# The last 52 rows of two neighbouring Z blocks in one buffer, contracted two at a time

## The chip, the cores and the metric

The kernel runs on one core of one Trainium2 chip. The metric is the device time of one execution in microseconds (us), as the median of several. Runs of the kernel before gave 372.31 us (371.18 to 373.6, three runs). A difference of about 1% is what such a measurement tells from none.

The core has five engines that run their own instruction streams and wait for one another through semaphores. In the profile PE is the matrix engine (TensorE), PEld its weight loads, DVE the vector engine, ACT the scalar engine, POOL the GpSimd engine, and SP the engine that only issues DMAs here. Matrix products are written to PSUM, eight banks of 512 fp32 columns, and read from there by DVE and ACT.

## The reference

Eight batches of 5696 positions and 128 channels go through a long convolution, done with Fourier transforms, and then through a spectral mixing layer with 64 modes:

```python
Yf = rfft(x, n=2*S, axis=1) * rfft(h, n=2*S, axis=0)[None]
x  = irfft(Yf, n=2*S, axis=1)[:, :S, :]
X  = rfft(x, axis=1)
Yr = einsum(Xr, w_r) - einsum(Xi, w_i)          # the first 64 modes alone
Yi = einsum(Xr, w_i) + einsum(Xi, w_r)
y  = irfft(Y, n=S, axis=1)
u  = x + y
out = u + maximum(u @ w_ch, 0)
```

Inputs and output are fp32; the kernel works in fp16 with fp32 sums.

## The kernel before

The length 5696 is written as 89 x 64 (NQ x J). The transforms are matrix products with constant tables in two steps. The batches go in four groups of two (`g_`).

**First part, 0 to 249 us.** For each group, PE makes a first transform over the 89 (`a_tile`, buffers As), then in ticks of four frequencies a second one over the 64 (`second`: matmuls that contract 64 rows, the two batches on partitions 0-63 and 64-127 in turn, `As,M`; the filter's own are `Ah,M`). DVE multiplies by the filter (`products`, U), PE transforms back one step (`U,Wc`), ACT copies the result to Zs or Zt, and SP stores it to a scratch in HBM (`zscr`). Matmuls `G,Zs` take the 64 modes from the same data. `modes` and `second` follow one another in each tick.

**Second part, the output stage, 249 us to the end.** The scratch is read back in 16 Z blocks, four for each group. A block holds, for 16 of the 64 inner positions, all 2 x 90 = 180 rows of frequency (real and imaginary) of two batches: 128 rows of 8 KB go to a buffer ZTa (1024 KB), the 52 rows 128 to 179 to partitions 32 to 83 of a buffer ZTb (416 KB). Partitions 0 to 31 of ZTb are cleared by POOL (`clear_zt`), since those matmuls contract partitions 0 to 83 with the first 32 zero. There are five rooms of such pairs (`NC = 5`); block i + 5 is sent for (`load_zt`, on SP's queue) when the last tile of block i has been issued (b equal to 1).

A Z tile (`u_tile`, `u_z`) is half a block of one batch and fills two PSUM banks of 356 columns. For each bank PE runs one matmul of 356 columns (`u_c`: the mixing layer's share, `IBs,C`), and then four times one of 128 rows (`S4a,ZTa`) and one of 84 rows (`S4b,ZTb`), each 89 columns. ACT or DVE then copies both banks to UT. There are 64 such tiles. Between them stand the result tiles (`o_tile`): four matmuls of 256 columns with the channel weights (`WI,UT`), a ReLU on ACT (R), a sum on DVE (O), and, after every second one as a rule, a DMA of 512 KB to the output. O has seven rooms of 512 KB, used in turn, and four smaller ones. All loads of Z and all stores of results go through SP's one queue, in program order.

Which order the instructions have is written out by hand. During the last group's ticks a table `early` says at which tick a load is issued: tick 8 loads the table S4b, 10 block 0, 12 S4a, 14 the table IBs, 16 block 1, 19 block 3, 21 block 2; block 4 follows at the end. Only the first 33 of 64 columns' groups of S4a, S4b and IBs are loaded; the rest is made from them on the chip (`reflect`, lines 545 to 552: S4a and IBs on DVE, S4b on ACT). Three Z tiles (block 0) are run without their `IBs,C` matmuls ahead of time, between the matmuls of the mixing layer (`mix`).

All matmuls have line 323 in the profile (the helper `mm`), all DMAs line 320, ACT's copies line 311, DVE's line 315.

Of the kernel before, what the change touches and what calls it, by code (L numbers as in the profile page):

```python
# [4 lines left out]
P = 128  # L5
# [118 lines left out]
def bass_long_conv_fft__then__afno_spectral_mix_kernel(nc, x, h, moe_w_r, moe_w_i, moe_w_ch, out):  # L124
# [37 lines left out]
    s4t = np.zeros((P, 2 * SH))  # L162
    s4t[:, 0:SH] = rows[0:P, 0:SH]
    s4t[PB:PB + RB, SH:2 * SH] = rows[P:2 * NK, 0:SH]
    sg = np.ones((P, 3))
    sr = np.stack([(-1.0) ** kk, -(-1.0) ** kk], axis=1).reshape(2 * NK)
    sg[:, 0] = sr[0:P]
    sg[PB:PB + RB, 1] = sr[P:2 * NK]
    sg[M:P, 2] = -1.0
    tt = np.arange(S)  # L170
# [79 lines left out]
    wc_sb = at("Wc", 2 * P, F16, take(2 * P * 2))  # L250
    sg_sb = at("SG", 3, F32, take(12))
# [4 lines left out]
    ZB = 16  # L256
# [4 lines left out]
    zt_off = [(a_h, a_h2), (a_as1, a_as1 + 2 * ZP), (a_as1 + 4 * ZP, a_as1 + 6 * ZP), (a_h + 2 * ZP, a_h2 + 2 * ZP),  # L261
              (a_m2, a_g)]
    assert 2 * S + 8 * ZP <= AW * 2
    zt = [[at(f"ZT{i}{'ab'[p_]}", ZP, F16, zt_off[i][p_]) for p_ in range(2)] for i in range(NC)]
    ib_sb = at("IBs", S, F16, a_m)
    s4_sb = [at("S4a", S, F16, a_m + 2 * S), at("S4b", S, F16, a_as)]
    assert 4 * S + 2 * ZP + 4 * P + 2048 <= 2 * MW
# [31 lines left out]
    def bank(i):  # L299
        return ("bank", i)  # L300
# [226 lines left out]
    ZX = [("zs", i, b) for i in range(NZ, NZL) for b in range(2)]  # L527
    zt_old = [(H_ALL, H_ALL), (AST, AST), (AST, AST), (H_ALL, H_ALL), (M_ALL[3:6], G_ALL)]

    def load_zt(i):  # L530
        g_, c_ = divmod(i, J // ZB)
        for part, (p0, r0, n) in enumerate(((0, 0, P), (PB, P, RB))):
            old = list(once(("zt", i % NC, part), zt_old[i % NC][part]))
            dma("sync", bass.AP(zt[i % NC][part], p0 * ZP, [[ZP, n], [1, ZP]]),
                bass.AP(zs, (g_ * 2 * NK + r0) * J * 256 + c_ * ZB * 256, [[J * 256, n], [1, ZP]]),
                "t", [("zd", g_, s_) for s_ in range(NT)], [("zt", i % NC, part)], after=old)

    def clear_zt(i):
        z32 = zt[i][1][0:PB, :].bitcast(U32)
        R.add("gpsimd", lambda e: e.memset(z32, 0), (), [("zt0", i)], after=list(zt_old[i][1]) + pace)  # L540

    def load_ib():
# [11 lines left out]
    def load_s4(part):  # L554
        n = PB + RB if part else P
        dma("sync", s4_sb[part][0:n, 0:SH], bass.AP(c_s4, part * SH, [[2 * SH, n], [1, SH]]), "p", (),
            [("s4", part, 0)], after=AST if part else M_ALL[1:4])
# [13 lines left out]
    pace = []  # L571

# [176 lines left out]
    for g_ in range(NP):  # L749
        if g_ == NP - 1:  # L750
            load_w(0)
            load_w(1)
        for t in range(NT + LM):
            tick(g_, t)
            assert g_ + 1 < NP or not wp
            if g_ == NP - 1 and t in early:
                pace[:] = [("u", min(t, NT - 1) % NU)]
                early[t]()
        evac(bass.AP(xt, 2 * g_ + B, [[B * XTW, P], [B, 2], [3 * B, M], [1, 2]]), pv(MB, 0, [[M, 2], [1, M], [P, 2]]),
             [bank(MB)], [("xt", g_)], 1.0 / 64, eng="scalar", after=[("ag", k) for k in range(NS + 2 * XN, NK)])  # L760
        evac(bass.AP(xt, 2 * g_, [[B * XTW, P], [3 * B, M], [1, 2]]), pv(MB, M, [[1, M], [P, 2]]),
             [bank(MB)], [("xtn", g_)], -1.0 / 64, eng="vector" if g_ + 1 == NP else "scalar", after=[("ag", k) for k in range(NS + 2 * XN, NK)])
        if g_ + 1 < NP:
            for j in range(NB_, 32):
                a_tile(j, [(0, 4, 2, 6)[(j - 5) % 4]], "both" if j == 31 else (A, V)[(j - NB_) % 9 % 2])
                if j == 31:
                    second(g_ + 1, 0, 0, DA)
                if wp and j % 2 == 1:
                    dst, src_, ring, tok = wp.pop(0)
                    dma("gpsimd", dst, src_, ring, (), [tok], after=[("as", j)])  # L770


    pace[:] = []
    load_wi()
    for i in range(4, NC):
        load_zt(i)
        clear_zt(i)

# [4 lines left out]

    def u_z(i, b, half, alone=False, parts=(0, 1)):
        g_, c_ = divmod(i, NCH)
        t = ahead.get((i, b, half))
        if t is None:
            t = turns("l", LSLOT)
        z = zt[i % NC]
        for hb in parts:  # L790
            if not alone:
                u_c(i, b, half, t, hb, True)
            for pl in range(4):
                for ri in range(2):
                    pz = half * 8 + hb * 4 + pl
                    so = (c_ * ZB + pz) * NQ
                    n = (P, PB + RB)[ri]
                    mm(pv(t + hb, pl * NQ, [[1, NQ]]), z[ri][0:n, pz * 256 + b * P:pz * 256 + b * P + P], s4_sb[ri][0:n, so:so + NQ],
                       alone and pl == 0 and ri == 0, not alone and pl == 3 and ri == 1, [("zt", i % NC, ri), ("zt0", i % NC), ("s4", ri, 0)] + ([("s4", ri, 1)] if c_ >= NCH // 2 else []), [bank(t + hb)])
        if alone:  # L800
            ahead[(i, b, half)] = t
        return t

    def u_c(i, b, half, t, hb, first_):
        g_, c_ = divmod(i, NCH)
        pl0 = half * 8 + hb * 4
        mm(pv(t + hb, 0, [[1, 4 * NQ]]), c_sb[:, (2 * g_ + b) * P:(2 * g_ + b + 1) * P],
           ib_sb[:, (c_ * ZB + pl0) * NQ:(c_ * ZB + pl0 + 4) * NQ], first_, not first_,
           [("c", g_ // 2), ("ib", 0)] + ([("ib", 1)] if c_ >= NCH // 2 else []), [bank(t + hb)])

    def u_tile(i, b, half):
        g_, c_ = divmod(i, NCH)
        t = ahead.get((i, b, half))
        if t is None:
            t = u_z(i, b, half)
        else:
            for hb in range(2):
                u_c(i, b, half, t, hb, False)
# [39 lines left out]
    reflect("vector", ib_sb, P, 2, ("ib",), M_ALL[0:2])  # L858

# [52 lines left out]
    todo = []  # L912
    NB = NCH * NP
    NW4 = NW // 4
    for g_ in range(NP):
        last = g_ == NP - 1
        order = [(c_, b) for b in range(2) for c_ in range(NCH)] if last else [(c_, b) for c_ in range(NCH) for b in range(2)]
        for n, (c_, b) in enumerate(order):
            i = NCH * g_ + c_
            for half in range(2):  # L920
                u_tile(i, b, half)
                for _ in range((2, 2 + half)[n >= NCH] if last else 1 + half):
# [4 lines left out]
            if last and n == NCH - 1:  # L927
                todo += [(g_, 0, r4) for r4 in range(NW4)]
# [37 lines left out]
```

## Time and profile before

| | value |
|---|---|
| median of three runs | 372.31 us |
| span of the profiled execution (first to last instruction) | 370.1 us |
| PE busy | 354.7 us (96%) |
| ACT busy | 316.2 us (85%) |
| DVE busy | 291.8 us (79%) |
| DMA, mean over the span | 281 GB/s |
| granted TensorE clock | 0.999 |
| Z tile evacuations, ACT and DVE | 46 of 752 ns, 18 of 892 ns |
| result stores O, 512 KB | 39, median 10.5 us from issue to landing |

The page and the trace are of one execution; the page gives its span and no separate total. A row of a timeline is: start in us from the span's first instruction, duration in us, engine, line, operation, output and inputs, shape and count; in brackets the engine's idle time before it and what ended that. Matmuls are pipelined and their ends are modelled, so what one costs is read from start to start. A row of DMA issues gives the count, the size of one in KB (1024 bytes) and the median time from issue to landing.

### The profile page before, as it was taken

Reading aid. Unit: us, or ns where it says so; the run is one execution under the profiler, and the core shown is the slowest. Engines: PE = TensorE matmul, PEld = TensorE weight load, DVE = VectorE, ACT = ScalarE, POOL = GpSimd, SP = SyncE. Lnnn points to the kernel's source line nnn. Section 1 sums busy time; section 2 is a strip of 40 time slices with the busy share of each in tenths; the row PEclk is TensorE's granted clock in tenths of the full one; section 3 lists DMA queues with packets and bytes.
Section 4 is the critical chain, followed back from the end, with each engine's and each line's share of the span. In section 5 each row is a group of like instructions: output and inputs, shape, how many; then the busy total and the mean of one; then the engine's idle time right before and its main releaser. Section 6 shows DMA issues by size and latency. Waiting matters only on the chain.

```text
span 370.1 us, 12455 instructions
## 1 busy us (share of the span) xinstructions
PE 354.7 (96%) x5350; PEld 276.5 (75%) x5350; DVE 291.8 (79%) x332; ACT 316.2 (85%) x499; POOL 75.2 (20%) x117
## 2 busy tenths in 40 slices
PE   7999899999999999999999999999999999999994
PEld 7878766667866668866668766668899888888873
DVE  3549899988999999989999988775357777756666
ACT  8559999999999999999999999995467777688885
POOL 8804012100833311823213001151000000000000
PEclk9999999999999999999999999999999999999999
DMA  7999979969999996999996999999999999999878
GB/s 139 209 271 382 249 165 292 232 198 283 93 140 213 263 258 186 132 160 215 263 278 128 171 310 363 342 345 388 381 410 386 413 410 408 418 399 376 326 291 349
DMA packets 87048, 103.94 MB, mean 281 GB/s; under 512 B 22730, under 2 KB 72522, under 8 KB 83438
## 3 DMA queue, kind: packets, MB, share of 16 engines
q1 hardware_dynamic: 64610, 81.33, 62.5%
q0 software_dynamic: 22384, 21.83, 35.4%
q8 instruction: 42, 0.69, 0.7%
q14 instruction: 12, 0.10, 0.1%
HBM read 70.61 MB, written 51.12 MB: 329 GB/s over the span
## 4 chain that ended last, share of the span: by engine, by line
PE 78%; ACT 10%; DMA 7%; DVE 3%; issue 1%; POOL 1%; DVEq 0%; POOLq 0%
PE ps L323 78%; ACT As L313 6%; DMA out_dram<-O 5%; DMA Hin<-in_h_dram 2%; ACT R L898 1%; DVE As L317 1%; ACT Xs L311 1%; DVE U L623 1%; POOL Hin L320 1%; ACT UT L311 1%; DVE O L899 0%; ACT Zs L311 0%; DVE Hp L438 0%; ACT C L313 0%; DVE Hs L315 0%
## 5 line engine op out<-in xcount | busy, mean ns | idle before, releaser
L652 DVE TENSOR_TENSOR U<-Xs,Hs 128x2048 f16<-128x2048 f16 (+1 forms) x72 | 85.8, 1197 | 12.1 <-ACT Xs L311 11.5
L323 PE MATMUL ps<-U,Wc 128*128 128x512 f16 (+1 forms) x368 | 93.8, 376 | 1.4 <-DVE U L623 1.4
L311 ACT CAST Xs<-ps 128x1024 f16<-128x1024 f32 (+1 forms) x76 | 75.0, 995 | 5.8 <-PE ps L323 3.1
L311 ACT CAST Zs<-ps 128x512 f16<-128x512 f32 (+1 forms) x132 | 70.1, 605 | 0.7
L899 DVE TENSOR_TENSOR O<-ps,R 128x512 f32<-128x512 f32 x81 | 52.4, 684 | 21.6 <-ACT R L898 11.4
L898 ACT ACTIVATE R<-ps 128x512 f32<-128x512 f32 (+1 forms) x92 | 50.5, 592 | 8.5 <-PE ps L323 8.4
L317 DVE TENSOR_SCALAR As<-ps 128x720 f16<-128x720 f32 x64 | 53.1, 879 | 4.8 <-PE ps L323 3.3
L323 PE MATMUL ps<-As,M 64*128 64x128 f16 (+3 forms) x1504 | 52.5, 214 | 2.4 <-ACT As L313 1.2
L313 ACT ACTIVATE As<-ps 128x720 f16<-128x720 f32 (+1 forms) x68 | 48.2, 771 | 5.0 <-PE ps L323 4.8
L323 PE MATMUL ps<-F,Xin 128*128 128x180 f16 x512 | 52.1, 249 | 0.1
L323 PE MATMUL ps<-WI,UT 128*128 128x256 f16 x360 | 50.8, 278 | 0.5 <-ACT UT L311 0.4
L311 ACT CAST UT<-ps 128x712 f16<-128x712 f32 x46 | 34.5, 752 | 19.4 <-PE ps L323 18.4
L323 PEld LDWEIGHTS ps<-U,Wc 128*128 128x128 f16 x368 | 29.1, 97 | 28.2 <-DVE U L623 1.9
L323 PEld LDWEIGHTS ps<-F,Xin 128*128 128x128 f16 x512 | 45.2, 155 | 6.7 <-DVE Xin L365 0.9
L323 PEld LDWEIGHTS ps<-As,M 64*128 64x128 f16 x1504 | 42.2, 94 | 8.7 <-ACT Xs L311 1.9
L323 PEld LDWEIGHTS ps<-WI,UT 128*128 128x128 f16 x360 | 38.9, 152 | 3.2 <-issue 1.8
L323 PE MATMUL ps<-IBs,C 128*128 128x356 f16 x128 | 39.2, 314 | 0.8 <-DVE O L899 0.7
L320 POOL DMA_DIRECT2D Xt<-in_x_dram x40 | 21.4, 540 | 76.5 <-PE ps L323 76.0
L323 PEld LDWEIGHTS ps<-G,Zs 128*128 128x128 f16 x512 | 26.1, 96 | 14.1 <-ACT Zs L311 0.2
L652 DVE TENSOR_TENSOR U<-ps,Hs 128x2048 f16<-128x2048 f32 (+1 forms) x16 | 35.5, 2216 | 0.0
L323 PE MATMUL ps<-G,Zs 128*128 128x128 f16 (+2 forms) x512 | 31.9, 192 | 0.1
L311 ACT CAST Zt<-ps 128x512 f16<-128x512 f32 x52 | 29.1, 659 | 0.0
(76 smaller groups left out, 479.4 us busy)
## 6 DMA issues: line engine op xcount, KB each, us to landing
out_dram<-O SPq DMA_DIRECT2D x39, 512.0 KB, 10.5
zscr<-Zs SPq DMA_DIRECT2D x62, 256.0 KB, 6.7
zscr<-Zt SPq DMA_DIRECT2D x26, 256.0 KB, 6.6
Xt<-in_x_dram POOLq DMA_DIRECT2D x20, 320.0 KB, 6.9
W<-wscr SPq DMA_DIRECT2D x4, 1024.0 KB, 8.5
ZT0a<-zscr SPq DMA_DIRECT2D x4, 1024.0 KB, 11.0
M<-cM POOLq DMA_DIRECT2D x5, 720.0 KB, 17.6
ZT1a<-zscr SPq DMA_DIRECT2D x3, 1024.0 KB, 11.1
```

The source lines that it names most:

```text
L311: R.add(e, lambda h_: h_.copy(dst, src), reads, writes, after=after)
L313: R.add(e, lambda h_: h_.activation(dst, src, COPY, scale=scale), reads, writes, after=after)
L317: R.add(e, lambda h_: h_.tensor_scalar_mul(dst, src, scale), reads, writes, after=after)
L320: R.add(eng, lambda h_: h_.dma_start(dst, src), reads, writes, ring=ring, after=after)
L323: R.add("tensor", lambda h_: h_.matmul(o, l, r, start=st, stop=sp), reads, writes)
L623: R.add("vector", lambda e: e.tensor_tensor(bass.AP(u_s[0], b * 512 + d0, [[2048, P], [1024, 2], [D, n], [1, d1 - d0]]), bass.AP(s_[0], s_ ...
L652: R.add("vector", lambda e: e.tensor_tensor(uv, src, hv, MULT), bk + [("h", t, 0), ("h", t, 1, 0), ("h", t, 1, J)], [("u", i)])
L898: R.add("scalar", lambda e: e.activation(rv, src_r, RELU), bk, [("r", i % NR)], after=once(("r", i % NR), G_ALL + XTT + [("y", 0), ("y", 1 ...
L899: R.add("vector", lambda e: e.tensor_tensor(ov, src_u, rv, ADD), bk + [("r", i % NR)], [key + (h_,)], after=once(key, old))
```

## The change

Blocks are handled in neighbouring pairs (2k and 2k + 1), `k` counting pairs. The 128-row parts have seven rooms of their own (ZA), the 52-row parts three rooms (ZB), each of which holds the 52 rows of both blocks of a pair: the even block's on partitions 0 to 51, the odd block's on 64 to 115. The table S4b is laid out to match, with all its columns loaded (128 partitions of 2848 columns, in place of 84 of 2937), and it isn't reflected any more. Nothing has to be cleared.

A tile now takes four inner positions of each of the two blocks, in place of eight of one. Its order on PE is: both `IBs,C` matmuls, the four 128-row matmuls of the first bank, the four of the second, and then four times one 52-row matmul of the even block into the first bank and one of the odd block into the second. The loads at a pair's end are both parts of ZB for pair k + 3 and ZA for blocks 2k + 7 and 2k + 8. In the early table, tick 10 sends for ZA0 and ZB0, 16 for ZA1, 19 for ZA2 and ZB1, 21 for ZA3; at the end follow ZA4, ZB2, ZA5 and ZA6. Result tiles stand at the same places between the tiles.

```diff
-    RB, PB = 2 * NK - P, 32
+    RB, PB = 2 * NK - P, 64
+    s4b = np.zeros((P, S // 2))
+    for p0 in range(2):
+        s4b[p0 * PB:p0 * PB + RB] = rows[P:].reshape(RB, J // ZB // 2, 2, ZB * NQ)[:, :, p0].reshape(RB, S // 2)
...
-    NC = 5
+    NCA, NCB = 7, 3
...
+    za_off = [a_h, a_as1, a_h + 2 * ZP, a_as1 + 4 * ZP, a_as1 + 6 * ZP, a_m2, a_g]
+    zb_off = [a_h2, a_h2 + 2 * ZP, a_as1 + 2 * ZP]
...
+    def load_za(i):
+        g_, c_ = divmod(i, J // ZB)
+        r_ = i % NCA
+        dma("sync", za[r_][:, :], bass.AP(zs, g_ * 2 * NK * J * 256 + c_ * ZP, [[J * 256, P], [1, ZP]]),
+            "t", zdone(g_), [("za", r_)], after=once(("za", r_), za_old[r_]))
+
+    def load_zb(k):
+        r_ = k % NCB
+        for p0 in range(2):
+            g_, c_ = divmod(2 * k + p0, J // ZB)
+            n = RB - RS
+            dma("sync", bass.AP(zb_[r_], p0 * PB * ZP, [[ZP, n], [1, ZP]]),
+                bass.AP(zs, (g_ * 2 * NK + P) * J * 256 + c_ * ZP, [[J * 256, n], [1, ZP]]),
+                "t", zdone(g_), [("zb", r_, p0)], after=once(("zb", r_, p0), zb_old[r_]))
-    def clear_zt(i):
-        z32 = zt[i][1][0:PB, :].bitcast(U32)
-        R.add("gpsimd", lambda e: e.memset(z32, 0), (), [("zt0", i)], after=list(zt_old[i][1]) + pace)
...
-             9: lambda: clear_zt(0),
-             10: lambda: load_zt(0),
+             10: lambda: (load_za(0), load_zb(0)),
              12: lambda: load_s4(0),
-             14: lambda: (load_id(), load_ib(), clear_zt(1)),
-             16: lambda: load_zt(1),
-             19: lambda: (load_zt(3), clear_zt(3)),
-             NT - 2: lambda: (load_zt(2), clear_zt(2))}
+             14: lambda: (load_id(), load_ib()),
+             16: lambda: load_za(1),
+             19: lambda: (load_za(2), load_zb(1)),
+             NT - 2: lambda: load_za(3)}
...
-    for i in range(4, NC):
-        load_zt(i)
-        clear_zt(i)
+    load_za(4)
+    load_zb(2)
+    load_za(5)
+    load_za(6)
...
+        if not alone:
+            for hb in range(2):
+                u_c(k, b, h4, t, hb, True)
+        for hb in range(2 if 0 in parts else 0):
+            z, r_ = za[(2 * k + hb) % NCA], (2 * k + hb) % NCA
             for pl in range(4):
...
+                mm(pv(t + hb, pl * NQ, [[1, NQ]]), z[:, pz * 256 + b * P:pz * 256 + b * P + P], s4_sb[0][:, so:so + NQ],
+                   alone and pl == 0, False, [("za", r_)] + ns, [bank(t + hb)])
+        for pl in range(4 if 1 in parts else 0):
...
+            for hb in range(2):
+                r0 = hb * PB
+                mm(pv(t + hb, pl * NQ, [[1, NQ]]), zb_[r_][r0:r0 + RB, pz * 256 + b * P:pz * 256 + b * P + P],
+                   s4_sb[1][r0:r0 + RB, so:so + NQ], False, not alone and pl == 3,
+                   [("zb", r_, hb), ("s4", 1, 0)], [bank(t + hb)])
...
-        evac(bass.AP(u_sb[ub], c_ * ZB + half * 8, [[S, P], [J, NQ], [4, 2], [1, 4]]),
-             src, [bank(t), bank(t + 1)], [("u_", ub, 2 * c_ + half)], eng=e, after=once(("u", ub), old))
+        evac(bass.AP(u_sb[ub], c_ * ZB + h4 * 4, [[S, P], [J, NQ], [ZB, 2], [1, 4]]),
+             src, [bank(t), bank(t + 1)], [("u_", ub, 2 * c_ + h4)], eng=e, after=once(("u", ub), old))
...
-    reflect("scalar", s4_sb[1], PB + RB, 1, ("s4", 1), AST)
...
-            if b == 1 and i + NC < NB:
-                load_zt(i + NC)
+            if b == 1:
+                if k + NCB < NPR * NP:
+                    load_zb(k + NCB)
+                for i in (2 * k, 2 * k + 1):
+                    if i + NCA < NCH * NP:
+                        load_za(i + NCA)
```

More of the change, by code (lines that the diff above doesn't have):

```diff
@@ L250, in bass_long_conv_fft__then__afno_spectral_mix_kernel @@
     wc_sb = at("Wc", 2 * P, F16, take(2 * P * 2))
-    sg_sb = at("SG", 3, F32, take(12))
+    sg_sb = at("SG", 2, F32, take(8))
     XTW = 3 * M
@@ L527, in bass_long_conv_fft__then__afno_spectral_mix_kernel, with zdone @@
     ZX = [("zs", i, b) for i in range(NZ, NZL) for b in range(2)]
-    zt_old = [(H_ALL, H_ALL), (AST, AST), (AST, AST), (H_ALL, H_ALL), (M_ALL[3:6], G_ALL)]
-    def load_zt(i):
-        g_, c_ = divmod(i, J // ZB)
[L532 to L536, printed above, removed]
-    def clear_zt(i):
-        z32 = zt[i][1][0:PB, :].bitcast(U32)
-        R.add("gpsimd", lambda e: e.memset(z32, 0), (), [("zt0", i)], after=list(zt_old[i][1]) + pace)
+    za_old = [H_ALL, AST, H_ALL, AST, AST, M_ALL[3:6], G_ALL]
+    zb_old = [H_ALL, H_ALL, AST]
+    def zdone(g_):
+        return [("zd", g_, s_) for s_ in range(NT)]
+    def load_za(i):
+        g_, c_ = divmod(i, J // ZB)
+        r_ = i % NCA
[9 more added lines that the diff above has]
+                "t", zdone(g_), [("zb", r_, p0)], after=once(("zb", r_, p0), zb_old[r_]))
     def load_ib():
@@ L782, in bass_long_conv_fft__then__afno_spectral_mix_kernel, with u_z @@
     ahead = {}
-    def u_z(i, b, half, alone=False, parts=(0, 1)):
-        g_, c_ = divmod(i, NCH)
-        t = ahead.get((i, b, half))
+    def u_z(k, b, h4, alone=False, parts=(0, 1)):
+        g_, c_ = divmod(2 * k, NCH)
+        t = ahead.get((k, b, h4))
         if t is None:
             t = turns("l", LSLOT)
[L789 to L792, printed above, removed]
-            for pl in range(4):
[L794 to L799, printed above, removed]
+        if not alone:
+            for hb in range(2):
+                u_c(k, b, h4, t, hb, True)
+        ns = [("s4", 0, 0)] + [("s4", 0, 1)] * (c_ >= NCH // 2)
+        for hb in range(2 if 0 in parts else 0):
+            z, r_ = za[(2 * k + hb) % NCA], (2 * k + hb) % NCA
+            for pl in range(4):
+                pz = h4 * 4 + pl
+                so = ((c_ + hb) * ZB + pz) * NQ
+                mm(pv(t + hb, pl * NQ, [[1, NQ]]), z[:, pz * 256 + b * P:pz * 256 + b * P + P], s4_sb[0][:, so:so + NQ],
+                   alone and pl == 0, False, [("za", r_)] + ns, [bank(t + hb)])
+        r_ = k % NCB
+        for pl in range(4 if 1 in parts else 0):
+            pz = h4 * 4 + pl
+            so = (c_ // 2 * ZB + pz) * NQ
+            for hb in range(2):
[3 more added lines that the diff above has]
+                   [("zb", r_, hb), ("s4", 1, 0)], [bank(t + hb)])
@@ L809, in u_c, with u_tile @@
            [("c", g_ // 2), ("ib", 0)] + ([("ib", 1)] if c_ >= NCH // 2 else []), [bank(t + hb)])
-    def u_tile(i, b, half):
-        g_, c_ = divmod(i, NCH)
-        t = ahead.get((i, b, half))
+    def u_tile(k, b, h4):
+        g_, c_ = divmod(2 * k, NCH)
+        t = ahead.get((k, b, h4))
         if t is None:
-            t = u_z(i, b, half)
+            t = u_z(k, b, h4)
         else:
             for hb in range(2):
-                u_c(i, b, half, t, hb, False)
+                u_c(k, b, h4, t, hb, False)
@@ L916, in bass_long_conv_fft__then__afno_spectral_mix_kernel @@
         last = g_ == NP - 1
-        order = [(c_, b) for b in range(2) for c_ in range(NCH)] if last else [(c_, b) for c_ in range(NCH) for b in range(2)]
+        order = [(c_, b) for b in range(2) for c_ in range(NPR)] if last else [(c_, b) for c_ in range(NPR) for b in range(2)]
         for n, (c_, b) in enumerate(order):
[L919 to L922, printed above, removed]
+            k = NPR * g_ + c_
+            for h4 in range(4):
+                u_tile(k, b, h4)
+                for _ in range((2, 2 + h4 % 2)[n >= NPR] if last else 1 + h4 % 2):
                     if todo:
                         o_tile(*todo.pop(0))
-            if b == 1 and i + NC < NB:
-                load_zt(i + NC)
-            if last and n == NCH - 1:
+            if b == 1:
[4 more added lines that the diff above has]
+                        load_za(i + NCA)
+            if last and n == NPR - 1:
                 todo += [(g_, 0, r4) for r4 in range(NW4)]
```

39 lines of the change are left out of this document (16 added, 23 removed).

## The prediction

> **What bounds the kernel now.** I read the page first, then busy time by stage, then TensorE's timeline inside one tile of the output stage, then the DMA issues one by one. The page: PE is busy 96% of the span and the chain that ended last is mostly PE.
>
> ```profile
> PE 354.7 (96%) x5350; PEld 276.5 (75%) x5350; DVE 291.8 (79%) x332; ACT 316.2 (85%) x499; POOL 75.2 (20%) x117
> DMA  7999979969999996999996999999999999999878
> PE 78%; ACT 10%; DMA 7%; DVE 3%; issue 1%; POOL 1%; DVEq 0%; POOLq 0%
> ```
>
> The change only touches what happens after 215 us, and its matmuls all lie in the output stage, 249 us to the end. The stage table (window: length, PE, PEld, DVE, ACT, POOL, clock, DMA share, GB/s):
>
> ```profile
> 275.00:300.00 25.00, 25.00 (x359) 22.43 (x357) 18.62 (x28) 17.96 (x31) 0.00 (x0) 1.00 1.01 403
> 335.00:350.00 15.00, 14.11 (x181) 12.26 (x180) 9.05 (x15) 12.41 (x23) 0.00 (x0) 1.00 0.93 372
> 350.00:370.00 20.00, 14.43 (x142) 11.44 (x139) 13.58 (x23) 14.05 (x25) 0.00 (x0) 0.99 0.77 306
> ```
>
> Two things are full at once until about 350 us: PE, and the DMA engines at 403 GB/s. So two questions decide: what a tile costs PE, and whether the DMAs that feed it come in time.
>
> **PE's cost per tile, before.** One tile of Z is two matmuls of 356 columns and sixteen of 89, in turn 128 rows (S4a) and 84 rows (S4b).
>
> ```profile
> 290.69 0.20 PE L323 MATMUL ps<-S4a,ZT2a 128*128 128x89 f16 x1
> ...
> 290.98 0.20 PE L323 MATMUL ps<-S4b,ZT2b 84*128 84x89 f16 x1
> 291.03 0.31 PE L323 MATMUL ps<-IBs,C 128*128 128x356 f16 x1
> ```
>
> From the first to the eighth start is 0.29 us, 7 steps: 42 ns a matmul, whether of 128 or 84 rows. A tile has 8 of the short ones: 8 x 42 = 336 ns. There are 64 tiles (16 Z blocks, two images, two halves).
>
> **PE's cost per tile, after.** The 8 short ones become 4 pairs, one on rows 0-51, one on rows 64-115, into two banks. The kernel already has such pairs: As,M and Ah,M contract 64 rows, on alternating halves.
>
> ```profile
> 123.14 0.22 PE L323 MATMUL ps<-G,Zt 128*128 128x128 f16 x1
> 123.29 0.28 PE L323 MATMUL ps<-As,M 64*128 64x128 f16 x4
> ...
> 124.13 0.22 PE L323 MATMUL ps<-As,M 64*128 64x128 f16 x2
> 124.28 0.11 PEld L323 LDWEIGHTS ps<-U,Wc 128*128 128x128 f16 x2
> 124.28 0.39 PE L323 MATMUL ps<-U,Wc 128*128 128x512 f16 x1
> ...
> 53.72 0.41 PE L323 MATMUL ps<-Ah,M 64*128 64x64 f16 x16
> 53.97 0.61 PE L323 MATMUL ps<-As,M 64*128 64x128 f16 x16
> ```
>
> The As,M run of 32 (16 pairs) starts at 123.29 and its last two start together at 124.13: 15 periods in 0.84 us, 56 ns a pair at 128 columns. Ah,M: 8 pairs in 0.25 us, 31 ns at 64 columns. At 89 columns I take 42 ns a pair, what one such matmul takes now (straight line between the two: 41), with ends 31 and 56. Pairing by itself so saves 336 - 4 x 42 = 168 ns a tile, 64 x 168 = 10.8 us.
>
> But the same rows show what it costs to go in and out. The last G,Zt starts at 123.14 and As,M only at 123.29: 150 ns. Where nothing changes but the weights, the same step is a third of that:
>
> ```profile
> 121.67 0.49 PE L323 MATMUL ps<-G,Zt 128*128 128x2 f16 x8
> 122.00 1.02 PE L323 MATMUL ps<-U,Wc 128*128 128x512 f16 x4
> 122.86 0.50 PE L323 MATMUL ps<-G,Zt 128*128 128x2 f16 x8
> 123.29 1.07 PE L323 MATMUL ps<-As,M 64*128 64x128 f16 x32
> ```
>
> The same eight G,Zt take 0.33 us up to U,Wc and 0.43 up to As,M: 0.10 us more. On the way out 124.13 to 124.28 is 150 ns where a pair takes 56, and the weights of U,Wc begin to load only at 124.28: again 0.095. The rows name no releaser there. So I price each change of row grouping at 95 ns. In this kernel the 84-row matmuls follow the 128-row ones at the plain 42 ns, so they pay none; the new ones pay two a tile, 190 ns, 64 x 190 = 12.2 us. The sum on PE is 12.2 - 10.8 = **+1.4 us**, with the ends of the pair's price (4 x 31, 4 x 56): 64 x (124 + 190 - 336) = -1.4 and 64 x (224 + 190 - 336) = +5.0.
>
> [...]
>
> **The DMAs.** The bytes are the same except S4b, which becomes 712 KB (128 rows of 2848) in place of 482 KB (84 of 2937): about 0.24 MB at 403 GB/s, 0.6 us of a queue that is full, at 224 us. What moves is the order, since a pair of Z blocks needs both halves at its first tile. Issues, start and duration on SP's queue, and the landing times of the same DMAs:
>
> ```profile
> 241.31 0.56 SPq L320 DMA_DIRECT2D ZT1a<-zscr  x1
> 257.67 2.29 SPq L320 DMA_DIRECT2D ZT4a<-zscr  x1
> 261.25 1.31 SPq L320 DMA_DIRECT2D ZT0a<-zscr  x1
> 264.05 0.35 SPq L320 DMA_DIRECT2D ZT1a<-zscr  x1
> ```
>
> ```profile
> ZT1a<-zscr SPq DMA_DIRECT2D x1, 1024.0 KB, 7.7
> ...
> ZT4a<-zscr SPq DMA_DIRECT2D x1, 1024.0 KB, 10.2
> ...
> ZT0a<-zscr SPq DMA_DIRECT2D x1, 1024.0 KB, 10.3
> ...
> ZT1a<-zscr SPq DMA_DIRECT2D x1, 1024.0 KB, 11.1
> ```
>
> They land at 249.0, 267.9, 271.6 and 275.2: one block (1024 + 416 KB) per 3.6 us, first in, first out. PE uses the blocks at these times:
>
> ```profile
> 262.39 0.20 PE L323 MATMUL ps<-S4a,ZT2a 128*128 128x89 f16 x1
> 262.63 0.21 PE L323 MATMUL ps<-S4b,ZT2b 84*128 84x89 f16 x1
> ...
> 270.46 0.20 PE L323 MATMUL ps<-S4a,ZT4a 128*128 128x89 f16 x1
> ...
> 277.16 0.20 PE L323 MATMUL ps<-S4a,ZT0a 128*128 128x89 f16 x1
> ```
>
> Block 4 (ZT4) is used at 270.46, block 5 (ZT0 again) only at 277.16, 5.5 us after it landed. Changed, the first tile of pair 2 needs block 5 too, at 270.46 + 0.15 (the second 356) + 4 x 0.042 = 270.8. Queue ahead of it: ZA4 and both halves of ZB2, one 416 KB half more than the 271.6 of today has (by size 1.0 of the 3.6 us): 272.0, where today's next half would end, to 272.6. With S4b's 0.6 us it lands at 272 to 273.2: **PE waits 1.2 to 2.4 us, I take 1.5**. In the same way block 1 is wanted by the stage's very first tile, near the 249.0 at which it lands today, and has one more half and the larger S4b ahead of it; and block 3, now the last of four in the queue, is wanted at 262.7, when today's last (ZT2b, for which PE waits from 262.39 to 262.63) comes. What PE loses there makes its wait for block 5 shorter by as much, so it isn't added.
>
> Then the results' rooms. A pair's end issues four loads at once (up to 2.9 MB) where each block's end issued 1.44 MB. Today the end of block 7, just before the results issued at 301.47, sends for block 12. The end of pair 3 (blocks 6 and 7) will send for ZA13, ZA14 and ZB6 (12 and 13), after ZA12: two loads of 1024 KB and one of 416 more are then in the queue ahead of those results, 2 x 2.6 + 1.0 = 6.2 us.
>
> ```profile
> 301.47 4.21 SPq L320 DMA_DIRECT2D out_dram<-O  x3
> ...
> out_dram<-O SPq DMA_DIRECT2D x1, 512.0 KB, 12.7
> ...
> 316.16 0.69 DVE L899 TENSOR_TENSOR O<-ps,R 128x512 f32<-128x512 f32 x1 [0.71 <-issue]
> ...
> 336.13 0.21 PE L323 MATMUL ps<-S4b,ZT0b 84*128 84x89 f16 x1 [0.16 <-DMA ZT0b<-zscr]
> ...
> 337.48 0.69 DVE L899 TENSOR_TENSOR O<-ps,R 128x512 f32<-128x512 f32 x1 [0.53 <-DMA out_dram<-O]
> ```
>
> The result issued at 301.47 lands at 314.2, and its room (seven O rooms, in turn) is written again at 316.16: 2.0 us to spare. With 6.2 us more in front and PE some 2 late by then, DVE waits about 2.2 us, and PE behind it as its four PSUM pairs fill: I take **+1.8 us**, bounds 0 (SP's own backpressure spaces the loads) and 4. That wait takes in what PE lost between 272 and 316. What is late today near 336, 0.5 us for the room and 0.2 for ZT0b, goes, since the last loads are issued one block earlier: -0.6 us. PE's cost after 318 us, 16 tiles x 22 ns, +0.4.
>
> **What costs nothing.**
>
> ```profile
> 249.47 2.60 ACT L550 ACTIVATE S4b<-S4b,SG 84x2759 f16<-84x2759 f16 x1
> 252.30 0.59 ACT L311 CAST Y<-ps 128x512 f16<-128x512 f32 x1 [0.24 <-PE ps L323]
> 249.19 1.83 POOL L540 MEMSET ZT4b<- 32x2048 uint32 x1
> ```
>
> ACT's reflection of S4b goes, but ACT then waits for PE (0.24 us) before its next instruction: 0 gained. The five memsets go from POOL, which has nothing later to do; no PE row waits for one. The evacuation's eight values per column come as two runs of four, 16 blocks apart instead of adjacent; same element count, I take 0.
>
> **Sum:** 1.5 + 1.8 + 0.4 - 0.6 = +3.1 us. The page gives this execution's span, 370.1, and no separate total; the median, 372.31, is 2.2 above it for what lies around the span. Both move by the same: 372.3 + 3.1 = **375.4 us**.
>
> **Rivals.** A, the forecast: the pairing pays for its own switches and the waits for block 5 and the rooms remain. Chance 0.52, 374 to 378.5.
> B, nothing: the queue is less strict than I read it, the loads come in time, and PE's +1.4 is partly taken back by the waits that go (0.6): 373.1. For it: today's waits for a Z load, at 262 and 336 us, are 0.2 us each. Chance 0.24.
> C, faster: a switch costs nothing between 89-column runs, because weights of the next group can load while few columns drain. PE would gain 10.8 us, but the DMA stays full: from 350 us on it moves 306 GB/s, so 6.1 MB need 15 us at 403, and the end comes no earlier than 5 us before today's; with waits for block 5 about 368. Against it: every entry and exit in the rows above, at 128 columns. Chance 0.10, half of it above 368.6.
> D, much slower: 52 rows don't run as pairs (they are no full 64), yet pay the switch: 64 x 190 = 12.2, less the waits that this hides, 384. It takes over from the waits (3.1 us) once a pair costs some 50 ns: 64 x (200 + 190 - 336) = 3.5. Against it: 64-row pairs start together. Chance 0.08.
> E, the change doesn't do what it says: the 52-row matmuls are issued as whole-array ones, no pair, no switch, 42 ns each; then PE is as before and the waits of A remain, 375. Chance 0.06.
>
> **The range.** 371 to 380 leaves out D and most of C; its top takes PE's +5.0 with the rooms' wait, its bottom B with the pair at 31 ns. About 1% (3.7 us) is what a measurement of this kernel tells from no change. Faster by more: half of C and a little of B's low side, 0.09. Slower by more (over 376.0): a good half of A (0.29), with D and 0.03 of E, 0.40. Within: 0.51.
>
> **What would show it.** S4b matmuls starting two at a time, about 42 ns a pair; 130 to 140 ns from the last S4a to the first S4b, and from the last pair to the next weights, once a tile. A PE wait for ZA at the third pair, near 272 us; DVE waits for O's landing near 318. DMA share still 1.0 until 350. I am wrong if the step into S4b is 42 ns, if PE waits for no Z load before 275, or if TensorE's tile time is off by more than 70 ns from today's.

## The result, and the profile after

The changed kernel takes **390.61 us** (median of four runs, 389.35 to 392.35) against 372.26 us for the kernel before beside it: a ratio of 1.0497, 95% interval [1.045, 1.0544]. That is 18 us slower. The forecast was 375.4 us, with a range that ended at 380. The span of the profiled execution went from 370.1 to 387.6 us. A few executions below, one of 645.76 us among them, ran over 1.5% longer than the fastest of their kernel: they count in the medians but not in the ratios, and no view of one is shown.

From the page of the changed kernel: TensorE's busy time, the granted clock and DMA share in 40 slices, and the chain that ended last.

```profile
PE 360.3 (93%) x5350; PEld 273.0 (70%) x5350; DVE 291.3 (75%) x332; ACT 314.0 (81%) x498; POOL 66.2 (17%) x112
PEclk9999999999999999999999999969999699999998
DMA  7999989967999999999978999999999999997768
PE 60%; DMA 20%; ACT 10%; DVE 4%; issue 2%; POOL 1%; SPq 1%; DVEq 0%; POOLq 0%
PE ps L325 60%; DMA out_dram<-O 10%; DMA ZA<-zscr 6%; ACT As L315 6%; DMA Xr<-in_x_dram 2%; DMA Xt<-in_x_dram 2%; ACT Xs L313 2%; ACT R L910 1%; DVE As L319 1%; POOL Hin L322 1%; DVE O L911 1%; DVE U L629 1%; SPq L322 1%; ACT UT L313 1%; DVE Xin L367 1%
```

PE's share of the chain fell from 78% to 60%, and the DMAs' rose from 7% to 20%: the stores of the results 10%, the loads of Z 6%. So the kernel now waits for transfers. In two slices the granted clock is 0.6. The reason shows when the output stage is cut into windows. The columns are the window, its length, the busy time of PE, PEld, DVE, ACT and POOL with instruction counts, the granted clock, the DMA share and GB/s. First the kernel before:

```profile
260.00:300.00 40.00, 39.97 (x615) 35.74 (x613) 24.52 (x35) 26.00 (x43) 0.00 (x0) 1.00 1.01 401
300.00:340.00 40.00, 39.13 (x540) 34.55 (x539) 27.04 (x41) 30.81 (x54) 0.00 (x0) 1.00 1.00 402
```

The same view of the kernel after, with two shorter windows:

```profile
260.00:300.00 40.00, 37.45 (x585) 29.80 (x581) 20.30 (x28) 22.69 (x36) 0.00 (x0) 1.00 1.01 345
300.00:340.00 40.00, 33.49 (x428) 27.04 (x429) 23.62 (x35) 21.37 (x37) 0.00 (x0) 0.91 1.00 370
250.00:260.00 10.00, 7.79 (x147) 6.95 (x148) 1.14 (x2) 2.63 (x6) 0.00 (x0) 0.66 1.07 301
300.00:310.00 10.00, 5.86 (x48) 4.30 (x49) 4.29 (x6) 1.89 (x4) 0.00 (x0) 0.66 1.02 372
```

**The engines of the DMA are as busy as before (1.01, 1.00), but they move 345 GB/s where they moved 401.** Each packet takes longer. In the trace, the 8 KB packets (one row of a Z block) took 309 ns in nearly every case before, 320 ns on average between 250 and 350 us. After the change the mean is 388 ns, and one in twenty takes 624 ns or more, twice the old time. The 4 KB packets of the results kept their 159 ns.

What PE then waits for, in order of time. From ScalarE's and TensorE's timelines of the kernel after (start, duration, instruction, count, and in brackets the idle time before it and what ended it):

```profile
250.16 1.66 ACT L313 CAST Zs<-ps 128x512 f16<-128x512 f32 x4 [2.65 <-DMA zscr<-Zs]
...
253.82 0.48 PE L325 MATMUL ps<-S4a,ZA 128*128 128x89 f16 x4 [1.22 <-DMA ZA<-zscr]
...
277.42 0.33 PE L325 MATMUL ps<-S4a,ZA 128*128 128x89 f16 x4
279.04 0.34 PE L325 MATMUL ps<-S4a,ZA 128*128 128x89 f16 x4 [1.29 <-DMA ZA<-zscr]
...
297.33 0.47 PE L325 MATMUL ps<-IBs,C 128*128 128x356 f16 x2
297.63 0.50 PE L325 MATMUL ps<-S4a,ZA 128*128 128x89 f16 x8
298.06 0.34 PE L325 MATMUL ps<-S4b,ZB 52*128 52x89 f16 x8
298.34 1.10 PE L325 MATMUL ps<-WI,UT 128*128 128x256 f16 x8
304.14 0.75 PE L325 MATMUL ps<-IBs,C 128*128 128x356 f16 x2 [4.71 <-DVE O L911]
...
336.30 0.46 PE L325 MATMUL ps<-IBs,C 128*128 128x356 f16 x2 [1.69 <-DVE O L911]
```

The waits are for a room behind a store of Z (2.65 us, through ScalarE), for block 1 (1.22), for block 5 (1.29), and twice for a result room (4.71 and 1.69). The first reaches TensorE as a pause of 2.3 us, by the list of waits (engine, line, what it waited for: us in total, times, the longest):

```profile
PE ps L325 <- ACT Zs L313: 2.3, 1, 2.3
```

With this pause and with the one of 4.71 us the clock was granted below full speed, which is the 0.66 of the windows 250 to 260 and 300 to 310: up to 0.34 x 10 = 3.4 us of full-speed time in each.

The 16 short matmuls of one tile behave nearly as forecast. The eight S4a start 43 ns apart; from the first S4b (298.06) to the start of the next matmul, with other weights (298.34), are 0.28 us. In the trace (medians of 61 tiles) the two matmuls of a pair start 3 ns apart and the four pairs 39, 56 and 42 ns apart, 46 ns on average; the step into them takes 136 ns, and the one out, from the last matmul of the last pair, 133 ns.

### The profile page after: what moved, and what is told of

It reads as the page before. It is cut to its first block, busy times and chain, and to the rows that moved or that the text cites. A ratio compares the mean times of both kernels' runs of the same rounds, so it can differ in the third digit from the quotient of the medians.

```text
span 387.6 us, 12443 instructions
## 1 busy us (share of the span) xinstructions
PE 360.3 (93%) x5350; PEld 273.0 (70%) x5350; DVE 291.3 (75%) x332; ACT 314.0 (81%) x498; POOL 66.2 (17%) x112
## 4 chain that ended last, share of the span: by engine, by line
PE 60%; DMA 20%; ACT 10%; DVE 4%; issue 2%; POOL 1%; SPq 1%; DVEq 0%; POOLq 0%
PE ps L325 60%; DMA out_dram<-O 10%; DMA ZA<-zscr 6%; ACT As L315 6%; DMA Xr<-in_x_dram 2%; DMA Xt<-in_x_dram 2%; ACT Xs L313 2%; ACT R L910 1%; DVE As L319 1%; POOL Hin L322 1%; DVE O L911 1%; DVE U L629 1%; SPq L322 1%; ACT UT L313 1%; DVE Xin L367 1%
## 5 line engine op out<-in xcount | busy, mean ns | idle before, releaser
L325 PE MATMUL ps<-WI,UT 128*128 128x256 f16 x360 | 53.1, 286 | 0.4 <-ACT UT L313 0.3
L325 PEld LDWEIGHTS ps<-S4a,ZA 128*128 128x128 f16 x512 | 29.6, 101 | 10.6 <-DMA ZA<-zscr 2.9
L325 PE MATMUL ps<-S4a,ZA 128*128 128x89 f16 x512 | 33.6, 209 | 3.2 <-DMA ZA<-zscr 2.5
L325 PE MATMUL ps<-IBs,C 128*128 128x356 f16 x128 | 30.0, 321 | 6.7 <-DVE O L911 6.4
```

The lines of the kernel that those rows point to most:

```text
L325: R.add("tensor", lambda h_: h_.matmul(o, l, r, start=st, stop=sp), reads, writes)
```

## The experiments

In the diffs `...` stands for lines that are not shown.

Two theories stood at the start. **P**: the 52-row loads are slow because of the partitions they go to (0-51 and 64-115 in place of 32-83). **Q**: they are slow because of the order and the burst of four loads at a pair's end.

**The place alone.** The kernel before with the 52 rows moved from partitions 32-83 to 0-51:

```diff
-        for part, (p0, r0, n) in enumerate(((0, 0, P), (PB, P, RB))):
+        for part, (p0, r0, n) in enumerate(((0, 0, P), (0, P, RB))):
...
```

> The kernel before with one thing moved: the 52 rows of every ZTb are loaded to partitions 0-51 in place of 32-83 (rows 52-83 are cleared, the table S4b has its rows moved to match). PE's instructions, bytes, order and rooms are those of before. Theory P (destination partitions: the SDMA engines that write a 52-row load get in each other's way when its rows lie on partitions 0-51, in each half of the changed kernel as well): the Z loads get slower as in the changed kernel, about 1 us a block, so 16 us less the 3 to 6 us of slack that the loads have, 380 to 388 us. Theory Q (order: four loads sent at once and two 52-row loads back to back are what slows the queue and starves PE): no change, 371 to 374 us.

Measured: 384.91 us, ratio 1.0347 [1.0299, 1.0395]. The order of the loads is that of the kernel before, and yet 13 us go. Its window of the output stage:

```profile
260.00:300.00 40.00, 35.84 (x556) 31.84 (x554) 20.70 (x29) 22.36 (x37) 0.00 (x0) 1.00 0.99 327
```

The DMAs are full at 327 GB/s. P holds, and Q alone can't explain this. (The edit also makes the first five small loads wait until POOL has cleared their rooms. The run with the pairs alone, further down, has the same wait with its loads at 32-83, and costs 0.7 us.)

**The odd half through another queue.** In the changed kernel the loads into 64-115 are issued by POOL:

```diff
-            dma("sync", bass.AP(zb_[r_], p0 * PB * ZP, [[ZP, n], [1, ZP]]),
+            dma("gpsimd" if p0 else "sync", bass.AP(zb_[r_], p0 * PB * ZP, [[ZP, n], [1, ZP]]),
```

> The changed kernel with the odd block's 52 rows (partitions 64-115) issued on POOL's DMA queue, the even block's still on SP's. Theory P: the two halves then run side by side on the engines and write different partitions, so about half of the collisions go: 376 to 384 us. Theory Q: the loads still come as a burst, and the results still queue behind them: 386 to 391 us.

Measured: 395.51 us, ratio 1.0636 [1.0576, 1.0696]. Both theories missed: it is slower still. Its window:

```profile
260.00:300.00 40.00, 38.29 (x636) 31.04 (x634) 19.69 (x28) 21.15 (x34) 1.55 (x3) 0.98 1.02 324
```

324 GB/s at a share of 1.02: the packets stayed long. Which part of the loss is the other queue's was not settled.

**Without the small loads, after and before.** The changed kernel without ZB's loads from pair 3 on, and the kernel before without ZTb's from block 5 on:

```diff
+        if k >= NCB:
+            return
```

```diff
+            if part and i >= NC:
+                continue
```

> The changed kernel without the ZB loads from the fourth pair on (pairs 3 to 7 contract what the three rooms hold from pairs 0 to 2; 4.3 MB of loads are left out). To be set beside the next one, which leaves out the same loads of the kernel before. PE's work is whole. My sum for PE gave +1.4 us for 64 tiles. Theory P: with no collisions after 275 us what is left over the next kernel is PE's 1 to 1.5 us and the late start of about 6: 6 to 9 us longer. Theory Q: the bursts of ZA and the results' rooms still make PE wait: 12 us or more.

> The kernel before without the ZTb loads from block 5 on (those blocks contract what the rooms hold; 4.7 MB of loads are left out). PE is the bound of this one: 0 to 3 us under the kernel before by both theories, 369 to 372 us.

Measured: 379.7 us, ratio 1.0224 [1.017, 1.0277], and 375.3 us, ratio 1.0102 [1.0038, 1.0166]. The second is a miss: taking 4.7 MB of transfers away does not make the kernel before faster. That TensorE bounds it would explain no gain; why it is 1% slower stays open. Between the two are 4.4 us, less than P had expected (6 to 9) and far from Q's 12. The unexplained 1% is part of this difference, so the pair says less than the next run.

**The same loads to all 128 partitions.** The changed kernel with each load of 52 rows of 8 KB (416 KB) replaced by one of 128 rows of 4 KB (512 KB, so 23% more bytes):

```diff
-            dma("sync", bass.AP(zb_[r_], p0 * PB * ZP, [[ZP, n], [1, ZP]]),
-                bass.AP(zs, (g_ * 2 * NK + P) * J * 256 + c_ * ZP, [[J * 256, n], [1, ZP]]),
+            dma("sync", bass.AP(zb_[r_], p0 * (ZP // 2), [[ZP, P], [1, ZP // 2]]),
+                bass.AP(zs, g_ * 2 * NK * J * 256 + c_ * ZP, [[J * 256, P], [1, ZP // 2]]),
...
```

> The changed kernel with each of the two 52-row ZB loads of a pair (52 x 8 KB) replaced by one of 128 rows x 4 KB to the same room, so that they write all 128 partitions (values are other rows of Z, so the 52-row products are not the reference's). Bytes per DMA engine, number of DMAs, bursts, rooms, order and PE are those of the changed kernel. Theory P: without the collisions only PE's switches (+1) and the earlier need for blocks 1, 3 and 5 and the burst are left: 374 to 379 us. Theory Q: as slow as the changed kernel, 386 to 391.

Measured: 375.73 us, ratio 1.0076 [1.0045, 1.0108]. Order, bursts, rooms and TensorE's work are those of the changed kernel, and nearly all of the loss is gone. From its windows and TensorE's timeline:

```profile
260.00:300.00 40.00, 39.96 (x610) 32.09 (x606) 23.81 (x34) 25.61 (x42) 0.00 (x0) 1.00 1.03 418
```

```profile
251.76 0.34 PE L325 MATMUL ps<-S4a,ZA 128*128 128x89 f16 x4 [0.38 <-DMA ZA<-zscr]
...
273.04 0.47 PE L325 MATMUL ps<-IBs,C 128*128 128x356 f16 x2
273.35 0.50 PE L325 MATMUL ps<-S4a,ZA 128*128 128x89 f16 x8
...
322.33 0.46 PE L325 MATMUL ps<-IBs,C 128*128 128x356 f16 x2 [1.44 <-DVE O L911]
```

The rate is 418 GB/s, the wait for a result room near 320 us is 1.44 us, the one for block 1 is 0.38, and there is none for block 5: the eight S4a matmuls of pair 2's first tile run through at 273.35. It is a near thing. The load of block 5 is the first of the two in this row, and lands 10.7 us after its issue:

```profile
262.29 0.97 SPq L322 DMA_DIRECT2D ZA<-zscr  x2
```

```profile
ZA<-zscr SPq DMA_DIRECT2D x1, 1024.0 KB, 10.7
```

That is 273.0 us, and the first matmul that reads it starts four steps after 273.35, at 273.5. In the changed kernel the same load was issued at 265.05 and landed 13.9 us later, at 279.0.

So 1.0497 - 1.0076 = 0.042 of 372.3 us, **about 15.7 us of the 18, hang on how the 52 rows are written**, and about 2.8 us ([1.7, 4.0]) on everything else.

The profiled executions differ before the output stage too. This is the same row of the last ticks in the kernel before, in the changed kernel, in this run and in the next one:

```profile
243.23 0.84 PE L323 MATMUL ps<-As,M 64*128 64x128 f16 x24
243.39 0.84 PE L325 MATMUL ps<-As,M 64*128 64x128 f16 x24
245.42 0.84 PE L325 MATMUL ps<-As,M 64*128 64x128 f16 x24
247.38 0.84 PE L323 MATMUL ps<-As,M 64*128 64x128 f16 x24
```

Against the kernel before, this run is 2.2 us late there and the next one 4.15, and in the traces they are so already at 213 us, where the kernels still do the same. So of the 3.9 us by which this run's span is longer (373.9 against 370.1) only 1.7 lie behind that point. Of the changed kernel's 17.5 us all but 0.2 do.

**TensorE's pairs alone.** The kernel before with the pair order of the change, on rows 0-51 and 64-115 of a room whose load is where it was:

```diff
...
+        for pl in range(4 if 1 in parts else 0):
+            for hb in range(2):
...
+                r0 = hb * 64
+                mm(pv(t + hb, pl * NQ, [[1, NQ]]), z[1][r0:r0 + RB, pz * 256 + b * P:pz * 256 + b * P + P],
+                   s4_sb[1][r0:r0 + RB, so:so + NQ], False, not alone and pl == 3, tok, [bank(t + hb)])
...
```

> The kernel before with PE's order of the changed one: per tile both IBs,C, eight 128-row matmuls, then four pairs of 52 rows (partitions 0-51 and 64-115 of ZTb, into two banks). Loads stay at partitions 32-83, one block at a time (so the 52-row products are of other rows than the reference's; rooms are cleared once, S4b is loaded in 128 rows). The forecast's PE sum: 64 x (4 x 42 + 190 - 336) = +1.4 us, 372.5 to 375. A rival by which pairs are worth their 2x and the change of row grouping is hidden by the short matmuls: up to 10.8 us less PE, with the DMAs full at best 365 to 368.

Measured: 373.65 us, ratio 1.002 [0.9985, 1.0054], that is +0.7 us and no measurable change. One of its tiles in TensorE's timeline:

```profile
290.15 0.47 PE L323 MATMUL ps<-IBs,C 128*128 128x356 f16 x2
290.45 0.50 PE L323 MATMUL ps<-S4a,ZT1a 128*128 128x89 f16 x8
290.88 0.34 PE L323 MATMUL ps<-S4b,ZT1b 52*128 52x89 f16 x8
291.16 0.66 PE L323 MATMUL ps<-WI,UT 128*128 128x256 f16 x4
```

1.01 us from the tile's first matmul to the next weights; the kernel before takes 0.98 (medians in the traces: 981 ns before, 1007 in the changed kernel). The pairs nearly halve the time of the S4b matmuls (four steps of 46 ns in place of eight of 43), and the two changes of row grouping (91 to 93 ns each beyond a plain step) take it back. The span of this profile is 5.9 us longer than that of the kernel before, of which 4.15 stand before the output stage (the row above); the 1.8 left are what 64 tiles at 26 ns make, 1.7.

**What about the place makes it slow?** Slow so far are rows 0-51 (1.0347), and 0-51 with 64-115 (1.0497); at 32-83 the same loads are fast. Is it partitions 0-31, or any other place than 32-83? The 52 rows went to 44-95, where 40 of them lie on partitions of the fast place:

```diff
-    RB, PB = 2 * NK - P, 32
+    RB, PB = 2 * NK - P, 44
...
```

> The kernel before with the 52 rows at partitions 44-95 (0-43 cleared) in place of 32-83. [...] If any start off a multiple of 32, or any other place than 32-83, is slow: 380 to 388.

Measured: 390.87 us, ratio 1.0452 [1.0395, 1.0509]. So it isn't partitions 0-31 alone that cost: this place shares 40 of 52 with the fast one and is no faster than 0-51 (1.0347 [1.0299, 1.0395]).

A new theory, **P2**, looks at who writes what: a load is slow when its DMA engines write other partitions than they write in a load to all 128. How many engines share a load can be estimated from the packet counts. The kernel without ZTb's last 11 loads has 715 packets fewer on SP's queue, 65 a load, which is 52 rows and 13 more:

```profile
q1 hardware_dynamic: 64610, 81.33, 62.5%
```

```profile
q1 hardware_dynamic: 63895, 76.64, 59.5%
```

(The first line is the kernel before, the second the one without the loads: packets, MB, share of the engines' time.) In the trace of the kernel before, that queue has 3790 packets of 4 bytes for its 240 DMAs, which comes out as 13 for each of the 16 loads of ZTb, 14 for S4b (84 rows) and 16 for each of the other 223. There are 16 engines on the page, so I take one such packet for one engine: 13 engines with four rows each for 52 rows. That is an estimate. Which engine takes which rows is not even that: no trace here names the engine of a packet. So what P2 foretells for a place or a cut below rests on an assumption of mine that no run shows.

**Same partitions, two cuts.** The kernel before with rows at 32-83 as ever, but each load cut in two: by rows (26 and 26), and as a control by columns (52 rows of half the length, twice).

```diff
-        for part, (p0, r0, n) in enumerate(((0, 0, P), (PB, P, RB))):
+        for q, (p0, r0, n) in enumerate(((0, 0, P), (PB, P, RB // 2), (PB + RB // 2, P + RB // 2, RB // 2))):
...
```

```diff
+        for q, (p0, r0, n, c0, w) in enumerate(((0, 0, P, 0, ZP), (PB, P, RB, 0, ZP // 2), (PB, P, RB, ZP // 2, ZP // 2))):
...
```

> The kernel before; each load of the 52 rows into partitions 32-83 is two loads of 26 rows (32-57 and 58-83). [...] Theory P2 (the loads are slow when an engine writes partitions that in a 128-row load belong to another engine): as slow as rows 0-51 and 44-95 were, 380 to 390 us, 8 KB packets again well over 309 ns. Rival Q2 (only the place counts: 32-83 is a good place whoever writes it): 371 to 374 us, packets at 309 ns.

> [...] Both theories: 371 to 375 us (the second issue costs SP under 1 us a block). If two loads for one are what costs, this one is as slow as the run before it.

Measured: by rows 393.02 us, ratio 1.048 [1.0387, 1.0572]; by columns 371.75 us, ratio 0.9986 [0.996, 1.0011]. The windows, first by rows, then by columns:

```profile
260.00:300.00 40.00, 33.51 (x497) 29.52 (x494) 17.06 (x24) 20.70 (x33) 0.00 (x0) 0.96 1.02 291
```

```profile
260.00:300.00 40.00, 40.00 (x625) 35.86 (x624) 24.54 (x35) 25.72 (x43) 0.00 (x0) 1.00 1.01 401
```

The same partitions, the same bytes and two loads in both: one costs 18 us, the other nothing. Place alone falls, and what P2 forecast came, though not shown to come by P2's reason.

**Rows 0-51 in two loads.** The 52 rows at 0-51 as loads of 32 and 20 rows, with the source written as eight and five groups of four. The aim was four rows an engine, by the estimate above, with five engines at work in both loads, an imbalance that has its price:

```diff
...
+                bass.AP(zs, ..., ([[4 * J * 256, n // 4], [J * 256, 4]] if q else [[J * 256, n]]) + [[1, ZP]]),
...
```

> [...] P2: 8 KB packets back near 309 ns, and a time below the 384.9 of rows 0-51, 372 to 380, by what the imbalance costs. Q2 (place alone): packets still up to 600 ns and 383 us or more.

Measured: 400.76 us, ratio 1.0716 [1.0654, 1.0779]: far from P2's 372 to 380, and within Q2's 383 or more. But the edit didn't do what it was meant to. Its line for SP's queue:

```profile
q1 hardware_dynamic: 64818, 81.33, 63.4%
```

That is 208 packets more than before, 13 for each of 16 blocks, so 26 beyond the 52 rows of a block and not 13: two rows for each and not four. The run doesn't test what it was made for.

**Another size.** 64 rows at 32-95, and at 64-127:

```diff
-    RB, PB = 2 * NK - P, 32
+    RB, PB, P0 = 2 * NK - P, 44, 32
...
-        for part, (p0, r0, n) in enumerate(((0, 0, P), (PB, P, RB))):
+        for part, (p0, r0, n) in enumerate(((0, 0, P), (P0, P + P0 - PB, RB + PB - P0))):
...
```

```diff
+    RB, PB, P0 = 2 * NK - P, 76, 64
...
```

> The kernel before with 64 rows in each second load, 116 to 179 (the first 12 again, against zeros in the table), at partitions 32-95; everything else as before. [...] P2: packets at 309 ns, 371 to 375 us. A rival that sees the trouble in any load at part of the partitions beyond 32-83: 380 us or more.

> The same 64 rows at partitions 64-127 (0-63 cleared, the contraction over 128 rows). [...] P2: slow, 380 to 395 us, packets well over 309 ns. A rival that blames the uneven load of 13 engines for the long packets: as fast as at 32-95, 371 to 375.

Measured: 372.28 us, ratio 0.9996 [0.9968, 1.0023], and 407.2 us, ratio 1.0885 [1.0798, 1.0972]. The windows, 32-95 first:

```profile
260.00:300.00 40.00, 39.58 (x614) 35.28 (x611) 23.84 (x35) 25.92 (x42) 0.00 (x0) 1.00 1.02 414
```

```profile
260.00:300.00 40.00, 28.25 (x419) 24.30 (x418) 13.45 (x18) 15.79 (x26) 0.00 (x0) 0.91 1.03 231
```

The two kernels load the same rows of the scratch (116 to 179) in loads of the same size, so what is read doesn't make the difference. 414 GB/s against 231: P2's direction again, at a size that none of the earlier runs had, though the loss is larger than the 395 us that I had put as its end. The loss needs no load of 52 rows, and so not the 13 engines of the estimate.

All together, with the mean and the 95th percentile of the 8 KB packets between 250 and 350 us from the traces:

```
small loads (rows x length, partitions)   ratio    GB/s 260-300   8 KB packets ns
52 x 8 KB, 32-83 (before)                 1        401            320, 322
2 x 52 x 4 KB, 32-83                      0.9986   401            325, 313
64 x 8 KB, 32-95                          0.9996   414            315, 322
128 x 4 KB, 0-127 (changed kernel)        1.0076   418            311, 309
52 x 8 KB, 32-83 (pairs alone)            1.002    388            333, 378
52 x 8 KB, 32-83, none from block 5 on    1.0102   373            361, 665
52 x 8 KB, 44-95                          1.0452   -              -
52 x 8 KB, 0-51                           1.0347   327            373, 618
52 x 8 KB, 0-51 and 64-115 (the change)   1.0497   345            388, 624
the same, odd half on POOL's queue        1.0636   324            392, 622
2 x 26 x 8 KB, 32-83                      1.048    291            426, 642
32 + 20 x 8 KB, 0-51                      1.0716   285            426, 732
64 x 8 KB, 64-127                         1.0885   231            488, 879
```

The first six rows, whose small loads start at 32 and are not cut by rows, or go to all 128 partitions, have a ratio of at most 1.0102 and a mean packet of 311 to 361 ns. The others have at least 1.0347 and, where there is a view, 373 to 488 ns. One row fits badly: the kernel whose small loads end with block 4 has long packets too (one in twenty 665 ns or more), though all its later loads are of 128 rows. So where and how the small loads are written is not the only thing that makes a packet long; what else does is open, and so is what sets the size of the loss. Why a packet takes longer at the slow places is not shown either. P2 fits the two cuts and the two places of the 64 rows in direction, but with its assumption on the engines it is argued and not shown.

No version here is measurably faster than the kernel before. The repair would be to load rows 0-51 and 64-115 at the full rate. I tried no such load of the right rows: the source rows of the two halves are not evenly spaced, so one strided load doesn't reach them, and cutting a load by rows gave 1.048 and 1.0716 above. With the loads at full rate (128 x 4 KB) the pairing still gains nothing.

## Why the prediction was wrong

- **The step that failed** is "The bytes are the same" and "What moves is the order", with "one block (1024 + 416 KB) per 3.6 us" carried over to the new partitions. The bytes were the same, but the engines moved 345 GB/s where they had moved 401. I had bounded the loads by their order in the queue alone, and put no price on the destination, though the change moves it. The rows in hand couldn't give one: all of the kernel's other loads of Z, and its own 52-row ones, were at good places (309 ns for nearly every packet of 8 KB). It was an operation that the trace of before does not show, and it should have had a bound of its own. In place of a block per 3.6 us, blocks 5 to 8 landed at 279.0, 283.6, 289.8 and 293.7 us, 4.9 us apart; with loads at full rate they landed 3.3 us apart (273.0 to 282.9). The step measures +15.7 us (1.0497 against 1.0076), or +13 alone in the kernel before.
- **TensorE's price was right.** Forecast 95 ns a switch, 42 ns a pair, +22 ns a tile, +1.4 us; measured 136 and 133 ns for the steps in and out (91 to 93 ns beyond a plain step), 46 ns a pair, +26 ns a tile, 64 x 26 = 1.7 us. Alone it is +0.7 us within [-0.6, +2.0].
- **The wait for block 5** came, 1.29 us against a forecast of 1.5, but for another reason: with the loads at full rate and the same order there is none, in the one execution profiled. There the block lands at 273.0 and TensorE needs it at 273.5. The whole execution is 2.2 us late from its first part; without that they would be 270.8 and 271.3, where the forecast had 272 to 273.2 and 270.8. So the order alone costs the block less than I took, and the 1.29 us come with the slow packets. A forecast number that is met isn't a reason confirmed.
- **The wait for a result room** was right as to its mechanism: 1.44 us near 320 us at full rate, against 1.8 near 318. At the slow rate it came earlier and larger, 4.71 at 304 and 1.69 at 336.
- **Block 1's wait**, which I didn't add, is 0.38 us at full rate and 1.22 in the changed kernel. I had put nothing on ScalarE's 2.65 us behind a store of Z; no such wait is among the waits of the kernel at full rate.
- **The granted clock** had no place in the forecast. The two pauses of 2.3 and 4.71 us came with windows at 0.66, so more was lost there than the length of the pauses.
- **The whole without the failed step**: the changed kernel with full-rate loads took 375.73 us. The forecast was 375.4. That they agree is in part luck: the parts were not all right (no wait for block 5, 1.5 too much; 0.4 for block 1), and in the profiled execution only 1.7 of the 3.9 us more lie in what the change touches, where 3.1 were forecast.
- **The rivals.** C falls: the switch takes 136 ns between 89-column runs as well. D's 384 us lies nearer to the result, but its mechanism is refuted, since 52-row matmuls do run as pairs, 46 ns each and the two starting 3 ns apart. E falls with the same rows. B's time is near that of the pairs alone (373.65), but not its condition, that the loads come in time.

## What to carry to other kernels

Where the DMA engines are full, as here from 260 to 340 us (a share of 1.0), a load of part of the partitions has a price to be measured: by its start and its cut the whole kernel took between nothing more (0.9986) and 8.9% more (1.0885). Fast here were the loads that start at 32 and are not cut by rows, and those to all 128 partitions. Look at GB/s beside the DMA share: the slowest kernel had a share of 1.03 at 231 GB/s, the one before 1.01 at 401. Pairing matmuls on two row groups pays only if a run is long enough to cover two changes of grouping: here four pairs of 89 columns save 4 x 40 ns (two steps of 43 against one of 46) and pay two switches of 91 to 93. When a change moves data to other partitions, price the transfer anew, even with the bytes unchanged.

## What the runs showed of the hardware that was not expected

- The same 52 rows at the same partitions, cut by rows into two loads: 1.048; cut by columns: 0.9986.
- A packet of 8 KB took 309 ns at good places and up to 879 ns (95th percentile, 64 rows at 64-127) at bad ones, while the DMA share stayed at 1.0. So the share alone doesn't tell how much the engines move.
- 4.7 MB fewer to load made the kernel before 1% slower and not faster ([1.0038, 1.0166]); not explained. In its profiled execution 3.9 of the 7.5 us more stand before 213 us already, where nothing is left out.
- Giving half of the small loads to POOL's queue cost a further 1.4% (1.0636 against 1.0497).
- With pauses of TensorE of 2.3 and 4.71 us the granted clock was 0.66 over ten microseconds; with pauses of 1.44 us (128 x 4 KB) the page's clock row shows no slice below 0.9 but the last. No limit follows: with rows 0-51 the window 290 to 300 has a pause of 2.38 us and a clock of 1.00, and 326 to 336 one of 2.24 us and a clock of 0.83.
